# A fused attention and feed-forward kernel: the last pairs' work behind the first late pair's x pieces

## The chip, the cores and the metric

The kernel runs on one core of a Trainium2 chip. The metric is the device time of one execution in microseconds (us). Before the change it was 1020.24 us, the median of three runs (1018.71 to 1024.19).

## The reference, cut to what matters

```
def phi(x):                                # q and k: 8 batches x 8 heads x 576 x 64
    proj = x @ w_phi                       # 64 -> 128 features
    proj = proj - max(abs(proj), axis=-1)
    return concat([exp(proj), exp(-proj)])
kv  = phi(k)^T v ;  z = sum(phi(k))        # per head
out = (phi(q) @ kv) / (phi(q) @ z + 1e-6)
x   = out as 4608 tokens x 512
h   = x @ w_in                             # 512 -> 2048
g   = max(h, 0) + alpha * min(h, 0)
return g @ w_out                           # 2048 -> 512
```

## The kernel before, in words

**Attention phase.** Two heads make a pair; there are 32 pairs, 0 to 31. A pair goes through slots: its features are projected (`pj`, `pl`), centred on VectorE (DVE), exponentiated on ScalarE (ACT), multiplied (`kv`, `n`, `d`), and its numerator `s` is copied by ACT. The denominator `ds` takes a way of its own: SyncE (SP) writes it out as 9 values per partition, DVE inverts it (`r9`), SP stores and reloads it spread over the partitions (`rec_d`, then `rr`), GpSimd (POOL) multiplies `s` by `rr` (function `finish`), and SP stores the product into `x_d` (`store`). Beside that, POOL, ACT and DVE decode the weights and split every number into a high part (a cast to fp32r) and a low part (a subtraction), so that each product is three matmuls: high by high, low by high, high by low. In the same phase the first 512 tokens go through the feed-forward layer (`h`, `o`, `os`); their rows of `x_d` are read back (`xr`), cast by ACT and given low parts by POOL (`first_x`).

**Late phase.** The other 4096 tokens are four late pairs of 512-token chunks, p = 1 to 4. For each, seven combinations of blocks (a Strassen-like scheme: A11, A12, S1 to S4, A22) replace eight. `prepare` loads x rows (`xr`, two loads j = 0 and 1 of 1 MB, issued by POOL) and makes the 14 pieces `xo`: a subtraction if need be, a cast (ACT), a low part (DVE; for p = 1 and j = 1 POOL). Then eight units multiply them by w_in (`pa`, `pb`, `pc`; `begin`, `second`, `rest`, `end`), and `down_pair` multiplies by w_out (`qa`, `qb`, `qc`), adds up and stores output tiles (`give`). The pieces for p + 1 are made while pair p runs.

**What sets the order.** Up to the turn to the late phase every step is put at a place in a list: slot plus an offset from the table `OFF` (one column per kind of slot). Each of the five engines executes its steps in the order of that list. An engine never skips ahead: SP waits for a store's data before it issues the load behind it, POOL waits for `rr` before a low part that stands behind the multiplication. TensorE (PE) has places of its own (`PE_AT`, `FIRST`). In the late phase PE, SP and POOL follow the order in the code; DVE and ACT are ordered by a scheduler when the program is built.

Names used below: `s28` is the numerator of pair 28, `rr28` its spread reciprocal; `xo1_7_1` is the low or high part of piece 7 (S4) of late pair 1, half j = 1, `xo1_1_1` that of piece 1 (A22); `xr2_0` are the rows of late pair 2, half 0. Line 225 is the low part, 221 the cast, 580 the multiplication by `rr`, 777 the load of `xr`, 743 the store of an output tile, 809 to 811 the three matmuls of a late product, 437 the projection, 509 the last transpose of q, 662 the sum `os`.

Of the kernel before, what the change touches and what calls it, by code (L numbers as in the profile page):

```python
# [8 lines left out]
F32 = mybir.dt.float32  # L9
# [7 lines left out]
P = 128  # L17
# [19 lines left out]
UX, UH = 2, 0  # L37
PIECES = [(k, u) for k in range(1, 7) for u in range(NU)][3 : 3 + 45 : 3]
# [33 lines left out]
    ds=(14.33, 13.3, 7.99, 15.45, 13.27, 9.58),
    d9=(16.85, 17.98, 14.45, 17.7, 21.14, 20.67),
    dv=(5.89, 1.69, 8.95, 10.25, 13.98, 16.22),
    rd=(10.99, 12.64, 11.51, 16.79, 32.02, 21.63),
    rr=(17.22, 17.27, 24.13, 23.33, 40.33, 27.36),
    x=(22.95, 34.89, 31.98, 25.08, 41.28, 35.09),
    xs=(14.53, 27.34, 32.32, 34.7, 31.02, 35.64),
    load=(11.94, 16.85, 8.08, 15.36, 6.2, 15.96),
    scale=(8.31, 4.75, 6.13, 7.61, 3.27, 8.3),  # L80
    split=(10.48, 10.24, 9.28, 10.06, 10.86, 11.57),
    rest=(12.11, 11.81, 10.23, 10.08, 13.2, 12.51),
    add=(13.68, 15.29, 13.93, 15.13, 16.68, 13.36),
    high=(16.18, 17.39, 22.06, 16.52, 18.18, 17.09),
    low=(25.11, 17.99, 23.95, 16.85, 21.91, 23.14),
    store=(35.74, 50.42, 20.3, 10.28, 50.84, 20.57),
    sum0=(20.35, 11.48, 6.28, 10.58, 10.81, 8.43),
    sum1=(25.64, 12.1, 7.59, 11.85, 12.61, 11.64),
    sum2=(29.45, 17.95, 14.72, 20.15, 16.27, 13.45),
    sum3=(35.42, 19.51, 23.09, 22.37, 20.63, 15.46),  # L90
    sum4=(45.71, 24.55, 30.48, 31.06, 27.55, 30.01),
# [12 lines left out]
    cx0=(10.38, 5.5, 5.5, 17.0, 5.5, 5.5),
    cx1=(14.08, 6.0, 6.0, 17.95, 6.0, 6.0),
    cx2=(18.53, 7.0, 7.0, 18.55, 7.0, 7.0),
    cx3=(18.59, 7.5, 7.5, 19.84, 7.5, 7.5),
    lx0=(22.77, 7.0, 7.0, 17.54, 7.0, 7.0),
    lx1=(17.8, 7.1, 7.1, 21.69, 7.1, 7.1),
    lx2=(21.35, 8.1, 8.1, 22.98, 8.1, 8.1),  # L110
    lx3=(22.81, 8.2, 8.2, 21.47, 8.2, 8.2),
    al=(-136.86, 8.5, 8.5, -54.87, 8.5, 8.5),
    pt0=(5.56, 5.6, 5.6, 10.71, 5.6, 5.6),
    pt1=(7.23, 6.3, 6.3, 12.6, 6.3, 6.3),
    pt2=(7.5, 7.0, 7.0, 14.91, 7.0, 7.0),
# [89 lines left out]
def fused_kernel(ctx: ExitStack, tc: tile.TileContext, kq, v, w_phi, w_in, w_out, alpha, out):  # L205
# [211 lines left out]
    def attention_units(i):  # L417
# [190 lines left out]
        put(i + 2, "x", finish)  # L608
        put(i + 3, "xs", store)
# [157 lines left out]
    def prepare(p):  # L767
        c = 2 * p - 1
        todo = []
        for j in range(2):  # L770
# [162 lines left out]
    def down_pair(p):  # L933
# [4 lines left out]
        for k, n in enumerate(ORDER):  # L938
# [4 lines left out]
            for u in range(NU):  # L943
# [4 lines left out]
                for m in range(2):  # L948
# [9 lines left out]
                    if u == NU - 1:  # L958
                        ps = bk[key, m]
                        if n == A11:  # L960
                            bk["b", m] = bank(1, f"qb{p}_{m}")
                            act.copy(bk["b", m], ps)
                            continue
                        i = goal[n][0] + m, goal[n][1]
                        cuts = (0, C2 // 2, C2) if last_pair and m and n == A22 else (0, C2)
                        if i in part:
                            added(part[i], ps, part[i])
                            give(*i, part[i])
                            continue
                        x = part[i] = out_tile(*i)  # L970
                        for a, b in zip(cuts, cuts[1:]):
                            if a:
                                dve.tensor_copy(x[:, a:b], ps[:, a:b])
                            else:
                                act.copy(x[:, a:b], ps[:, a:b])  # L975
                            if n in (A12, A22):
                                give(*i, x, (a, b))
# [12 lines left out]
    with tc.manual_schedule(engines={et.PE, et.SP, et.Pool}):  # L990
        for n, bufs in (("hv", 1), ("gs", 1), ("wv", 1)):
            late[n] = ctx.enter_context(tc.tile_pool(name=n + "p", bufs=bufs, reuse_waits="tile"))
        for p in range(1, NC2 // 2 + 1):
            more_pairs = p < NC2 // 2
            queue += [(p, k, u) for k in range(len(ORDER)) for u in range(NU)]
            for u in range(NU):
                if u == UX and more_pairs:
                    prep += prepare(p + 1)
                    pieces(1)
# [19 lines left out]
            if more_pairs:  # L1019
                load_up(p + 1, 0)  # L1020
# [43 lines left out]
```

## Time and profile before

| | |
|---|---|
| median of three runs | 1020.24 us |
| profiled execution | 1020.62 us, span 1018.8 us |
| PE busy | 997.8 us, 98% of the span |
| DVE, ACT, POOL busy | 72%, 59%, 28% |
| mean granted PE clock | 0.996 |

The profile cuts the span into 40 slices. PE is at 9 tenths or more in all but the first, the sixteenth (some 382 to 407 us) and the last; the granted clock is below 9 tenths only in the seventeenth (407 to 433 us). DMA engines are 60 to 80% busy in the attention phase. A wait costs the whole kernel something only if PE stands still for it; so the view of what PE waited for comes first, and the order of instructions around each of those waits second.

### The profile page before, as it was taken

The page shows a single profiled execution, that of the slowest core. Times are in us where ns is not written, and L with a number is a line of the kernel's source. Part 1 is how long each engine was busy: PE and PEld are TensorE (multiplying, and loading weights), DVE is VectorE, ACT ScalarE, POOL GpSimd, SP SyncE. Part 2 cuts the span into 40 slices and gives each one's busy share as a digit, 9 for nine tenths or more (in the row PEclk, how much of TensorE's full clock was granted, in tenths as well). Part 3 has the DMA queues.
Part 4 walks back from the last instruction along what each step waited for, and adds up shares of the span by engine and source line. Part 5 has one row for each costly group of instructions (what it writes and reads, how often), then busy time and mean ns, then how long its engine had stood idle before and what let it go on. Part 6 is the DMA issues. An engine that isn't in the chain of part 4 may idle for free. (4 is left out here: it accounts for less than half of the span.)

```text
span 1018.8 us, 20525 instructions
## 1 busy us (share of the span) xinstructions
PE 997.8 (98%) x8142; PEld 803.8 (79%) x8142; DVE 736.7 (72%) x1106; ACT 597.1 (59%) x1051; POOL 283.1 (28%) x255
## 2 busy tenths in 40 slices
PE   8999999999999998999999999999999999999997
PEld 7777777777777775888888788888788888888886
DVE  7898788989898666657963657973566973565863
ACT  5887777677676665446653446654445653444552
POOL 0478767878787426000001000001000001000001
PEclk9999999999999999899999999999999999999999
DMA  6689887888887876547666557666556666454564
GB/s 200 182 281 306 272 263 240 283 278 271 299 269 263 258 235 206 202 177 254 236 218 224 198 193 250 230 213 228 190 213 248 223 211 218 168 212 176 186 211 141
DMA packets 106512, 232.41 MB, mean 228 GB/s; under 512 B 16944, under 2 KB 37808, under 8 KB 100272
## 3 DMA queue, kind: packets, MB, share of 16 engines
q1 hardware_dynamic: 101376, 214.24, 63.1%
q0 software_dynamic: 4752, 16.78, 4.5%
q8 instruction: 65, 1.06, 0.4%
q14 instruction: 31, 0.25, 0.1%
q10 hardware_dynamic: 288, 0.07, 0.0%
HBM read 182.53 MB, written 48.38 MB: 227 GB/s over the span
## 5 line engine op out<-in xcount | busy, mean ns | idle before, releaser
L221 ACT CAST hv<-g 128x512 fp32r<-128x512 f32 x224 | 139.2, 623 | 121.8 <-DVE hv L225 60.4
L225 DVE TENSOR_TENSOR hv<-g,hv 128x512 fp32r<-128x512 f32 x224 | 153.8, 695 | 73.0 <-ACT hv L221 72.5
L743 POOL DMA_DIRECT2D out_dram<-pt x33 | 18.0, 546 | 355.0 <-ACT pt L975 273.3
L809 PE MATMUL qa<-hv,wv 128*128 128x512 f32 x256 | 99.6, 389 | 0.0
L810 PE MATMUL qa<-hv,wv 128*128 128x512 f32 x256 | 99.6, 389 | 0.0
L811 PE MATMUL qa<-hv,wv 128*128 128x512 f32 x256 | 99.6, 389 | 0.0
L456 DVE TENSOR_REDUCE m<-pj 128x8 f32<-128x1024 f32 x64 | 77.3, 1208 | 30.4 <-PE pj L437 30.3
L475 ACT ACTIVATE xk<-t 128x1024 f32<-128x1024 f32 x64 | 67.2, 1062 | 34.4 <-DVE t L457 34.4
L457 DVE TENSOR_TENSOR t<-pj,m 128x1024 f32<-128x1024 f32 x64 | 78.4, 1225 | 4.1 <-ACT xk L475 0.4
L485 PE MATMUL kv<-v,xk 128*64 128x65 f32 x2048 | 78.0, 223 | 0.0
L485 PEld LDWEIGHTS kv<-v,xk 128*64 128x64 f32 x2048 | 70.7, 138 | 4.0 <-issue 0.3
L437 PEld LDWEIGHTS pj<-w_sb,raw 64*128 64x128 f32 x1024 | 60.0, 188 | 13.0 <-issue 6.7
L777 POOL DMA_DIRECT2D xr<-x_d x8 | 6.0, 755 | 230.8 <-DVE xo L225 230.4
L437 PE MATMUL pj<-w_sb,raw 64*128 64x128 f32 x1024 | 66.7, 279 | 2.7 <-DVE os L662 1.4
L531 PE MATMUL n<-qf,sf 128*64 128x288 f32 x512 | 68.2, 407 | 0.6 <-issue 0.5
L829 ACT ACTIVATE r<-g 128x512 f32<-128x512 f32 x65 | 37.6, 625 | 51.2 <-DVE g L825 51.2
L292 POOL TENSOR_TENSOR a<-e,a 128x512 f32<-128x512 f32 x32 | 44.6, 1394 | 79.5 <-DVE e L288 78.9
L830 DVE SCALAR_TENSOR_TENSOR g<-r,aln,g 128x512 f32<-128x512 f32 x65 | 48.5, 783 | 19.6 <-ACT r L829 19.6
L580 POOL TENSOR_TENSOR s<-s,rr 128x576 f32<-128x576 f32 x32 | 47.8, 1495 | 36.7 <-DMA rr<-rec_d 29.6
L811 PEld LDWEIGHTS qa<-hv,wv 128*128 128x128 f32 x256 | 48.0, 188 | 10.2
L810 PEld LDWEIGHTS qa<-hv,wv 128*128 128x128 f32 x256 | 48.1, 188 | 10.0
L809 PEld LDWEIGHTS qa<-hv,wv 128*128 128x128 f32 x256 | 48.1, 188 | 9.8
(147 smaller groups left out, 2585.9 us busy)
## 6 DMA issues: line engine op xcount, KB each, us to landing
ws<-us_d SPq DMA_DIRECT2D x32, 1024.0 KB
wv<-vs_d SPq DMA_DIRECT2D x64, 512.0 KB
wv<-v_d SPq DMA_DIRECT2D x48, 512.0 KB
raw<-kq_dram SPq DMA_DIRECT2D x31, 576.0 KB
wa<-u_d SPq DMA_DIRECT2D x32, 512.0 KB
v<-v_dram SPq DMA_DIRECT2D x32, 320.0 KB
rr<-rec_d SPq DMA_DIRECT2D x64, 144.0 KB
x_d<-s SPq DMA_DIRECT2D x32, 288.0 KB
```

The lines of the kernel that those rows point to most:

```text
L221: return act.copy(dst, src)
L225: return eng.tensor_tensor(dst, src, f(hi), op=ALU.subtract)
L437: pe.matmul(dst, lhsT=c["raw"][hs, j * P : (j + 1) * P], rhs=w_sb[hs], start=True, stop=True)
L456: dve.tensor_reduce(m, src, axis=AX.X, op=ALU.max, apply_absolute_value=True)
L457: dve.tensor_tensor(dst, src, m.unsqueeze(3).broadcast_to([P, nh, nj, FD]), op=ALU.subtract)
L475: act.activation(c["x", 0][:, n], c["t", 0], AF.Exp, scale=(1.0, -1.0)[n])
L485: pe.matmul(t[D * g : D * g + D, a, h * (D + 1) : (h + 1) * (D + 1)], lhsT=c["x", ch][:, a, h, j, D * g : D * g + D], rhs=c["v"][:, n : n ...
L531: pe.matmul(ps[D * h : D * h + D, :], lhsT=c["st"][:, a, D * h + 1 : D * h + D + 1], rhs=c["qf"][:, h, a, u * HS : (u + 1) * HS], start=a ...
L809: pe.matmul(ps, lhsT=wh, rhs=xh, start=first, stop=False, skip_group_check=True)
L810: pe.matmul(ps, lhsT=wl, rhs=xh, start=False, stop=False, skip_group_check=True)
L811: pe.matmul(ps, lhsT=wh, rhs=xl, start=False, stop=end, skip_group_check=True)
L830: dve.scalar_tensor_tensor(g, r, al1[:, ff : ff + 1], src, op0=ALU.mult, op1=ALU.add)
```

## The change

It has five parts.

1. The table `OFF` has new numbers for nearly all steps of ACT, DVE, POOL and SP in the attention phase; `finish` and `store` of the last five pairs (27 to 31) get entries of their own. PE's order is the same, instruction for instruction.
2. In `prepare` for p = 1 the low part of a piece is put behind the cast of the next piece (`behind`).
3. The rows of late pair p + 1 are asked for in the down phase of pair p (`PIECES` begins with (0, 3)) and no longer in its third unit (`UX`).
4. The last pair's last output tiles leave on SP's and ACT's queues and no longer on POOL's; the last half tile has a tile of its own (`y_end`).
5. `give` has an argument for the queue.

```
-UX, UH = 2, 0
-PIECES = [(k, u) for k in range(1, 7) for u in range(NU)][3 : 3 + 45 : 3]
+PIECES = [(0, 3)] + [(k, u) for k in range(1, 7) for u in range(NU)][3 : 3 + 45 : 3]
...
-    cx0=(10.38, 5.5, 5.5, 17.0, 5.5, 5.5),
+    cx0=(13.63, 5.5, 5.5, 17.0, 5.5, 5.5),
...
+    x_e31=(49.08, 49.08, 49.08, 215.43, 49.08, 49.08),
+    xs_e31=(58.7, 58.7, 58.7, 243.8, 58.7, 58.7),
...
-        put(i + 2, "x", finish)
-        put(i + 3, "xs", store)
+        e = f"e{i}" if i >= NPAIR - 5 else 0
+        put(i + 2, "x", finish, e)
+        put(i + 3, "xs", store, e)
...
-    def give(m, c, t, cuts=(0, C2)):
+    def give(m, c, t, cuts=(0, C2), queue=pool):
         for a, b in zip(cuts, cuts[1:]):
-            pool.dma_start(out[m * P : (m + 1) * P, c * C2 + a : c * C2 + b], t[:, a:b])
+            queue.dma_start(out[m * P : (m + 1) * P, c * C2 + a : c * C2 + b], t[:, a:b])
...
-                low(pool if p == 1 and j else dve, t[:, 1], b[src], t[:, 0])
+                behind.append(lambda: low(pool if p == 1 and j else dve, t[:, 1], b[src], t[:, 0]))
                 xo[p, n, j] = (t[:, 0], t[:, 1])
+                made[0] += 1
+                while len(behind) > int(p == 1 and made[0] < 14):
+                    behind.pop(0)()
...
-                        cuts = (0, C2 // 2, C2) if last_pair and m and n == A22 else (0, C2)
...
+                        if last_pair and m and n == A22:
+                            half, y = C2 // 2, late["cp"].tile([P, C2], F32, tag="cp", name="y_end", bufs=6)
+                            act.copy(x[:, :half], ps[:, :half])
+                            dve.tensor_copy(y[:, half:], ps[:, half:])
+                            give(*i, x, (0, half), act)
+                            give(*i, y, (half, C2), nc.sync)
+                            continue
+                        act.copy(x, ps)
+                        if n in (A12, A22):
+                            give(*i, x, queue=nc.sync if last_pair and n == A22 else pool)
...
-                if u == UX and more_pairs:
-                    prep += prepare(p + 1)
-                    pieces(1)
...
             if more_pairs:
+                prep += prepare(p + 1)
                 load_up(p + 1, 0)
```

POOL at the turn to the late phase, before:

```order
L580 TENSOR_TENSOR s28_5563<-s28_5563,rr28_5719 128x576
L225 TENSOR_TENSOR xo1_4_1_5783<-xr1_1_5463,xo1_4_1_5783 128x512
L580 TENSOR_TENSOR s29_5694<-s29_5694,rr29_5786 128x576
L580 TENSOR_TENSOR s30_5752<-s30_5752,rr30_5803 128x576
L225 TENSOR_TENSOR xo1_7_1_5810<-xr1_1_5463,xo1_7_1_5810 128x512
L777 DMA xr2_0_5986<-x_d_57 128x2x1024
L580 TENSOR_TENSOR s31_5800<-s31_5800,rr31_5814 128x576
L225 TENSOR_TENSOR xo1_1_1_5825<-xr1_1_5463,xo1_1_1_5825 128x512
L777 DMA xr2_1_6579<-x_d_57 128x2x1024
```

And now:

```order
L234 TENSOR_TENSOR xo1_4_1_5784<-xr1_1_5464,xo1_4_1_5784 128x512
L589 TENSOR_TENSOR s28_5471<-s28_5471,rr28_5716 128x576
L589 TENSOR_TENSOR s29_5618<-s29_5618,rr29_5780 128x576
L589 TENSOR_TENSOR s30_5719<-s30_5719,rr30_5799 128x576
L234 TENSOR_TENSOR xo1_7_1_5802<-xr1_1_5464,xo1_7_1_5802 128x512
L234 TENSOR_TENSOR xo1_1_1_5819<-xr1_1_5464,xo1_1_1_5819 128x512
L787 DMA xr2_0_6489<-x_d_57 128x2x1024
L589 TENSOR_TENSOR s31_5787<-s31_5787,rr31_5809 128x576
L787 DMA xr2_1_6579<-x_d_57 128x2x1024
```

The multiplication of pair 28 went behind piece 4; that of pair 31, and the load of `xr2_0`, went behind the last piece, `xo1_1_1`. The multiplications of pairs 28 to 30 still stand ahead of piece 7.

ACT where the first 512 tokens' rows (`xr0`) are cast to `x0`, before:

```order
L273 ACTIVATE a1_1_1338<-raw2_1_1206 128x512
L221 CAST x0_0_1359<-xr0_0_1315 128x512
L541 COPY s6_1366<-n6_1306 128x576
L221 CAST x0_1_1395<-xr0_0_1315 128x512
L558 ACTIVATE ds6_1397<-d6_1326 128x288
```

And now:

```order
L282 ACTIVATE a1_1_1356<-raw2_1_1140 128x512
L550 COPY s6_1363<-n6_1314 128x576
L567 ACTIVATE ds6_1365<-d6_1331 128x288
L504 COPY sf7_1368<-kv7_1254 128x260
L528 ACTIVATE qf8_1371<-qt8_1_1344 128x512 x2
L528 ACTIVATE qf8_1371<-qt8_0_1343 128x512 x2
L532 ACTIVATE qf8_1371<-q28_1353 128x2x64 x2
L230 CAST x0_0_1380<-xr0_0_1299 128x512
L230 CAST x0_1_1382<-xr0_0_1299 128x512
```

The two casts went behind the copy of the denominator (`ds6`) and the exponentials of q (`qf8`).

DVE where the sums of the first chunk's outputs meet the projection of pair 16, before:

```order
L372 SCALAR_TENSOR_TENSOR g0_5_2576<-r0_5_2575,aln_81,g0_5_2576 128x512
L662 TENSOR_TENSOR os0_2_2145<-o0_1_2_2659,os0_2_2145 128x512
L662 TENSOR_TENSOR os0_3_2188<-o0_1_3_2666,os0_3_2188 128x512
L456 TENSOR_REDUCE m16_0_2726<-pj16_0_2700 128x8
L457 TENSOR_TENSOR t16_0_2725<-pj16_0_2700,m16_0_2726 128x1024
```

And now:

```order
L672 TENSOR_TENSOR os0_3_2221<-o0_1_3_2660,os0_3_2221 128x512
L672 TENSOR_TENSOR os0_2_2147<-o0_1_2_2653,os0_2_2147 128x512
L576 RECIPROCAL r9_12_2728<-d9_12_2595 128x9
L465 TENSOR_REDUCE m16_0_2774<-pj16_0_2692 128x8
L466 TENSOR_TENSOR t16_0_2773<-pj16_0_2692,m16_0_2774 128x1024
```

The two sums changed places (the bank of `o0_1_3` is the one that `pj16_0` is written to next), and the reciprocal of pair 12, which stood ahead of the decoding steps, comes behind them.

## Rows read from the trace of the kernel before

**Rows 1.** The page: busy time, and granted clock in 40 slices

```profile
PE 997.8 (98%) x8142; PEld 803.8 (79%) x8142; DVE 736.7 (72%) x1106; ACT 597.1 (59%) x1051; POOL 283.1 (28%) x255
...
PEclk9999999999999999899999999999999999999999
```

**Rows 2.** Waits of PE, longest in total first: us, times, longest

```profile
PE pa L811 <- POOL xo L225: 3.4, 1, 3.4
...
PE q L509 <- ACT ds L558: 2.1, 1, 2.1
PE pj L437 <- DVE os L662: 1.4, 3, 0.5
```

**Rows 3.** Windows of 2 us: engines' busy time, granted clock, DMA share, GB/s

```profile
408.00:410.00 2.00, 2.00 (x5) 1.61 (x6) 0.95 (x2) 0.60 (x1) 0.00 (x0) 0.50 0.94 330
410.00:412.00 2.00, 2.00 (x6) 1.52 (x6) 0.00 (x0) 0.60 (x1) 0.00 (x0) 0.50 0.98 386
412.00:414.00 2.00, 2.00 (x7) 1.56 (x6) 1.29 (x3) 0.19 (x1) 0.00 (x0) 0.53 0.78 227
```

**Rows 4.** Timeline at the turn: start, us, engine, line, operation [idle before, releaser]

```profile
399.15 0.62 ACT L221 CAST xo<-xr 128x512 fp32r<-128x512 f32 x1 [0.28 <-DVE xr L786]
399.26 1.82 POOL L580 TENSOR_TENSOR s<-s,rr 128x576 f32<-128x576 f32 x1 [3.05 <-DMA rr<-rec_d]
...
401.04 1.71 POOL L225 TENSOR_TENSOR xo<-xr,xo 128x512 fp32r<-128x512 f32 x1
...
402.70 0.76 POOL L777 DMA_DIRECT2D xr<-x_d  x1
...
402.81 0.50 PE L811 MATMUL pc<-xo,ws 128*128 128x512 f32 x1 [0.94 <-POOL xo L225]
...
404.07 0.40 PE L810 MATMUL pa<-xo,wb 128*128 128x512 f32 x1
...
406.10 1.70 POOL L225 TENSOR_TENSOR xo<-xr,xo 128x512 fp32r<-128x512 f32 x1
...
407.86 0.80 PE L811 MATMUL pa<-xo,wb 128*128 128x512 f32 x1 [3.39 <-POOL xo L225]
...
412.71 0.69 DVE L786 TENSOR_TENSOR t<-xr 128x512 f32<-128x512 f32 x1 [3.76 <-DMA xr<-x_d]
```

**Rows 5.** Timeline in late pair 2: load of pair 3's rows, DVE and PE behind it

```profile
555.81 0.72 POOL L777 DMA_DIRECT2D xr<-x_d  x1
...
563.74 0.69 DVE L786 TENSOR_TENSOR t<-xr 128x512 f32<-128x512 f32 x1 [3.13 <-DMA xr<-x_d]
...
568.78 0.50 PE L809 MATMUL pa<-xo,ws 128*128 128x512 f32 x1 [0.81 <-ACT u L821]
```

**Rows 6.** Timeline where the first chunk's x rows are cast

```profile
81.73 0.62 ACT L221 CAST x<-xr 128x512 fp32r<-128x512 f32 x1 [1.43 <-DMA xr<-x_d]
...
83.77 0.44 PE L509 MATMUL q<-ident,t 128*128 128x128 f32 x2 [2.05 <-ACT ds L558]
...
89.00 3.93 POOL L225 TENSOR_TENSOR x<-xr,x 128x512 fp32r<-128x512 f32 x3
...
93.62 0.40 PE L618 MATMUL h<-x,wo 128*128 128x512 f32 x1
```

**Rows 7.** Timeline where PE waits for the sum of the first chunk's outputs

```profile
176.59 1.28 DVE L662 TENSOR_TENSOR os<-o,os 128x512 f32<-128x512 f32 x2
...
177.92 2.06 PE L437 MATMUL pj<-w_sb,raw 64*128 64x128 f32 x32 [0.51 <-DVE os L662]
```

**Rows 8.** Timeline at the end

```profile
1013.02 0.39 PE L811 MATMUL qa<-hv,wv 128*128 128x512 f32 x1
1013.64 1.60 POOL L743 DMA_DIRECT2D out_dram<-pt  x3 [9.03 <-ACT pt L975]
1013.85 0.42 DVE L973 COPY pt<-qa 128x256 f32<-128x256 f32 x1 [5.86 <-ACT pt L975]
```

**Rows 9.** Waits of POOL

```profile
POOL s L580 <- DMA rr<-rec_d: 29.6, 7, 19.8
```

More of the change, by code (lines that the diff above doesn't have):

```diff
@@ L72 @@
[L72 to L91, printed above, removed]
@@ new lines @@
+    mq=(5.65, 8.07, 3.52, 6.75, 7.22, 3.12),
+    mt=(4.86, 2.88, 2.46, 6.03, 5.06, 2.97),
+    ke0=(3.3, 5.91, 6.78, 6.85, 8.67, 6.12),
+    ke1=(5.41, 6.03, 12.54, 11.88, 8.79, 12.37),
+    ke2=(7.09, 8.35, 7.1, 9.5, 14.22, 12.93),
+    kc=(12.14, 13.05, 8.76, 6.89, 12.71, 14.18),
+    qe=(13.33, 9.13, 10.11, 16.92, 10.06, 14.93),
+    s=(11.27, 6.54, 7.74, 13.22, 9.42, 8.5),
+    ds=(11.47, 8.24, 8.89, 15.42, 9.64, 11.15),
+    d9=(14.54, 19.27, 17.56, 21.35, 21.96, 21.93),
+    dv=(5.45, 11.6, 15.99, 14.46, 14.76, 11.65),
@@ new lines @@
+    rd=(7.95, 21.83, 17.98, 16.47, 24.89, 20.99),
+    rr=(15.39, 26.39, 27.13, 26.0, 34.39, 24.65),
+    x=(24.48, 35.74, 28.84, 25.08, 42.2, 28.46),
+    xs=(13.16, 28.07, 34.55, 29.11, 32.66, 36.9),
+    load=(3.65, 1.17, 13.81, 15.36, 7.54, -0.66),
+    scale=(8.93, 2.88, 5.69, 7.61, 0.04, 2.07),
+    split=(10.5, 10.82, 9.19, 10.06, 8.58, 11.96),
+    rest=(13.41, 11.6, 9.29, 10.08, 11.25, 13.83),
+    add=(14.55, 13.93, 15.05, 15.13, 17.01, 13.92),
+    high=(16.77, 15.99, 18.22, 16.52, 18.82, 17.92),
@@ new lines @@
+    low=(23.03, 18.12, 20.12, 16.85, 22.67, 18.1),
+    store=(49.69, 30.27, 48.27, 10.28, 57.31, 24.73),
+    sum0=(23.02, 9.13, 9.24, 10.58, 6.74, 9.22),
+    sum1=(26.57, 12.92, 14.6, 11.85, 7.93, 13.07),
+    sum2=(29.05, 14.4, 15.42, 20.15, 14.93, 15.86),
+    sum3=(35.6, 21.69, 17.89, 22.37, 21.99, 19.22),
+    sum4=(46.26, 28.41, 23.63, 31.06, 29.31, 32.32),
+    glu0=(12.7, 23.39, 10.84, 12.7, 20.72, 14.29),
+    glu1=(13.8, 23.55, 12.6, 13.8, 32.16, 24.23),
+    glu2=(0.5, 0.54, 18.6, 0.5, 13.11, 18.71),
@@ new lines @@
+    cx2=(14.97, 7.0, 7.0, 18.55, 7.0, 7.0),
+    cx3=(19.44, 7.5, 7.5, 19.84, 7.5, 7.5),
+    lx0=(15.22, 7.0, 7.0, 17.54, 7.0, 7.0),
+    lx1=(17.22, 7.1, 7.1, 21.69, 7.1, 7.1),
+    lx2=(19.11, 8.1, 8.1, 22.98, 8.1, 8.1),
+    lx3=(20.55, 8.2, 8.2, 21.47, 8.2, 8.2),
+    al=(-60.47, 8.5, 8.5, -54.87, 8.5, 8.5),
+    pt0=(5.56, 5.6, 5.6, 8.67, 5.6, 5.6),
+    pt1=(7.23, 6.3, 6.3, 11.58, 6.3, 6.3),
+    pt2=(7.5, 7.0, 7.0, 12.6, 7.0, 7.0),
+    pt3=(12.61, 11.2, 11.2, 17.37, 11.2, 11.2),
+    pt4=(12.93, 13.6, 13.6, 19.64, 13.6, 13.6),
@@ new lines @@
+    pt5=(18.82, 16.0, 16.0, 22.15, 16.0, 16.0),
+    pt6=(23.73, 18.3, 18.3, 30.05, 18.3, 18.3),
+    pt7=(26.97, 20.7, 20.7, 36.21, 20.7, 20.7),
+    pt8=(31.93, 23.1, 23.1, 36.99, 23.1, 23.1),
+    pt9=(37.24, 25.5, 25.5, 44.62, 25.5, 25.5),
+    pt10=(46.04, 27.9, 27.9, 45.2, 27.9, 27.9),
+    pt11=(48.22, 30.2, 30.2, 54.91, 30.2, 30.2),
+    pt12=(54.07, 32.6, 32.6, 65.15, 32.6, 32.6),
+    pt13=(95.83, 35.0, 35.0, 68.21, 35.0, 35.0),
+    pt14=(130.31, 37.4, 37.4, 118.78, 37.4, 37.4),
+    pt15=(177.59, 39.8, 39.8, 119.13, 39.8, 39.8),
@@ new lines @@
+    lu0=(16.03, 6.0, 6.0, 4.97, 6.0, 6.0),
+    lu1=(25.62, 6.2, 6.2, 28.44, 6.2, 6.2),
+    mk_s0=(0.13, 1.4, 1.4, 1.4, 1.4, 1.4),
+    mt_s0=(3.74, 2.8, 2.8, 2.8, 2.8, 2.8),
+    mq_s0=(12.58, 4.2, 4.2, 4.2, 4.2, 4.2),
+    mk_s1=(1.09, -5.6, -5.6, -5.6, -5.6, -5.6),
+    mt_s1=(-1.15, -4.2, -4.2, -4.2, -4.2, -4.2),
+    mq_s1=(6.77, 2.1, 2.1, 2.1, 2.1, 2.1),
+    mk_s2=(1.68, -7.0, -7.0, -7.0, -7.0, -7.0),
+    mt_s2=(3.68, 0.84, 0.84, 0.84, 0.84, 0.84),
+    mq_s2=(9.27, 0.98, 0.98, 0.98, 0.98, 0.98),
@@ new lines @@
+    mk_s3=(-2.65, -6.3, -6.3, -6.3, -6.3, -6.3),
+    mq_s3=(5.67, 2.1, 2.1, 2.1, 2.1, 2.1),
+    mt_s3=(7.32, 3.5, 3.5, 3.5, 3.5, 3.5),
+    ke0_s3=(-0.74, -1.4, -1.4, -1.4, -1.4, -1.4),
+    ke1_s3=(0.32, 0.0, 0.0, 0.0, 0.0, 0.0),
+    ke2_s3=(10.9, 5.6, 5.6, 5.6, 5.6, 5.6),
+    ke0_s0=(6.38, 3.5, 3.5, 3.5, 3.5, 3.5),
+    ke1_s0=(7.57, 5.6, 5.6, 5.6, 5.6, 5.6),
+    ke2_s0=(9.81, 7.7, 7.7, 7.7, 7.7, 7.7),
+    kc_s0=(0.57, 0.7, 0.7, 0.7, 0.7, 0.7),
+    ke0_s1=(1.78, 0.84, 0.84, 0.84, 0.84, 0.84),
@@ new lines @@
+    ke1_s1=(5.55, 1.4, 1.4, 1.4, 1.4, 1.4),
+    ke2_s1=(-0.64, 2.1, 2.1, 2.1, 2.1, 2.1),
+    qe_s0=(26.95, 18.2, 18.2, 18.2, 18.2, 18.2),
+    kc_s1=(4.39, -1.4, -1.4, -1.4, -1.4, -1.4),
+    qe_s1=(25.24, 23.1, 23.1, 23.1, 23.1, 23.1),
+    ke0_s2=(2.19, -0.7, -0.7, -0.7, -0.7, -0.7),
+    ke1_s2=(5.62, 0.0, 0.0, 0.0, 0.0, 0.0),
+    ke2_s2=(8.73, 2.8, 2.8, 2.8, 2.8, 2.8),
+    s_s0=(2.74, 3.5, 3.5, 3.5, 3.5, 3.5),
+    ds_s0=(6.19, 6.3, 6.3, 6.3, 6.3, 6.3),
+    qe_s2=(12.08, 11.9, 11.9, 11.9, 11.9, 11.9),
@@ L768, in prepare @@
         c = 2 * p - 1
-        todo = []
+        todo, behind, made = [], [], [0]
         for j in range(2):
@@ L970, in down_pair @@
                         x = part[i] = out_tile(*i)
[L971 to L977, printed above, removed]
+                        if last_pair and m and n == A22:
[8 more added lines that the diff above has]
+                            give(*i, x, queue=nc.sync if last_pair and n == A22 else pool)
     ahead = unit(1, 0)
```

111 lines of the change are left out of this document (26 added, 85 removed).

## The prediction

> **What bounds the kernel now.** I read the page first, then what PE waited for, then the timeline around each long wait with the order of the engines beside it. PE is busy for 997.8 of the span's 1018.8 us [rows 1], and this change leaves its instructions and their order alone. So it can gain only where PE stands still or runs at half clock, and it can lose wherever a moved step makes PE stand still anew. The list of PE's waits [rows 2] shows the few places: 3.4 us for one low part from POOL, 2.1 us for a denominator on ACT, 1.4 us in three pieces for the sums `os` on DVE.
>
> The largest is the turn to the late phase [rows 4]. POOL executes in order, and low parts that PE needs stand behind multiplications that nobody needs yet. The multiplication at 399.26 (`s30`) stood 3.05 us for `rr`; so the low part of piece 7 began only at 401.04, though its cast, which reads unsubtracted rows, did not wait for that, and PE waited 0.94 us until 402.81. Then POOL issued the load of pair 2's rows (402.70), waited for `rr31`, multiplied, and began the low part of the last piece, A22, at 406.10; PE waited 3.39 us until 407.86. The cast for this one was done at 399.15 + 0.62 = 399.77: POOL's order alone made it late. After the stop the windows from 408 to 414 show a granted clock of 0.50, 0.50 and 0.53 [rows 3]; 0.50 is the 1.2 GHz level. These six us did the work of 2 x 0.50 + 2 x 0.50 + 2 x 0.53 = 3.06 us, a loss of 2.94. The turn thus costs 0.94 + 3.39 + 2.94 = 7.27 us.
>
> **The change part by part.**
>
> *POOL at the turn.* `xo1_1_1` now follows `xo1_7_1`, ahead of the load and of `s31`. `s30` is still ahead of `xo1_7_1`, and the requests that lead to `rr30` hardly move, so I leave that wait at 0.94. POOL then ends `xo1_7_1` at 401.04 + 1.71 = 402.75 and `xo1_1_1` 1.70 later, at 404.45. PE's matmul before the one that reads it starts at 404.07, and the next would follow 0.25 later (the five from 402.81 to 404.07 come 0.25 apart), at 404.32; with the signal between the engines about 0.2 us of waiting is left of 3.39. With so short stops I expect no fall of the clock: after the stop of 2.05 us at 83.77 [rows 6] the slice of the page stays at 9 [rows 1]. So 7.27 - 0.94 - 0.2 = 6.1 us come free here, if nothing else is late.
>
> *What is late next: the rows of pair 2.* Their load is issued at about 404.5 and no longer at 402.70, while PE is some 7 us ahead. DVE has subtractions on these rows in its order; the scheduler put them five rows later than before, behind the sum on S3 of unit 1. Before, DVE stood 3.76 us until 412.71, 10.0 us after the issue [rows 4]; PE, at half clock, didn't feel it. In pair 2 DVE stood 3.13 us and PE lost 0.81 through ACT's copy `u` [rows 5]: some 2.3 us of DVE's standing are covered. Now PE goes through A12, S2, S1 and S3 of unit 1 (24 matmuls at 0.25) from 404.5 to 410.5, DVE ends the sum (0.7 us) at about 411.4, and the rows land between 404.5 + 7.9 = 412.4 (7.9 is pair 2's load, 555.81 to 563.74) and 414.5 (10.0 as before). DVE stands 1.0 to 3.1 us, PE 0 to 0.8. I take 0.6, nearer the upper end, as the crowd of loads is the same as before. Turn: 6.1 - 0.6 = 5.5 us. Bounds: 7.3 if nothing at all is late, 0 if another stop is as long and the clock falls again.
>
> *Low parts one piece later.* For pair 1 a subtraction and its cast get ahead of the preceding low part, by one DVE or POOL step. No wait of PE hangs on it but those above: nothing, and 0.7 us (one step of DVE) on either side.
>
> *Rows asked for in the down phase.* On POOL the loads for pairs 3 and 4 stand where they stood, behind the last output tiles of the pair before, and DVE's subtractions on them too. The load at 555.81 and the 0.81 us of PE behind it stay [rows 5]. Nothing.
>
> *The casts of the first chunk's rows.* ACT stood 1.43 us for the rows before the cast at 81.73; the copy of the denominator was behind it, and PE waited 2.05 us for the bank [rows 6]. The casts now follow that copy and q's exponentials, which hides their wait for the DMA. Next in line are the low parts that the first product `h` reads: POOL ended them at 89.00 + 3.93 = 92.93, and the first matmul on one started at 93.62. With PE 2.05 us earlier it comes at 91.57; POOL no longer puts two half-width sums of weights between these low parts; at a low part's 1.3 us for both it would be done near 91.6. That just fits: 1.9 us, between 0 and 2.05.
>
> *The sums `os`.* Two of them took 1.28 us, and PE waited 0.51 for the second, whose bank `pj16` needs [rows 7]. Now the needed one is first, 0.64 us earlier: the wait goes. The same exchange stands at a second of the three waits; at the third only a reciprocal leaves the way. I count 1.0 of 1.4 us; bounds 0 and 1.4.
>
> *The end.* PE's last matmul begins at 1013.02 and takes 0.39. POOL issued three stores from 1013.64 to 1015.24, and DVE's copy began only at 1013.85 because it stood behind ACT's copy into the same tile [rows 8]. With a tile of its own it starts about 0.4 earlier, and three stores on two other queues end their issue near 1014.3: 0.9 us. What follows an issue stays. Bounds 0 and 1.6, POOL's whole issue time. The Trainium skill (Trainium Kernel Development and Optimization, Key Constraints) says that issuing from several engines only saves the sequencer's issue time, since all use the same DMA engines. It also gives (DMA: Bandwidth & Descriptors, Latency and other measured facts) a first byte after about 1 us by GpSimd's queue and 0.6 by the others, so by the page's figures the gain would be an estimated 1.3 us. No run here shows a store of the hardware queues at the end.
>
> *The rest of the table.* Some 600 rows of ACT, DVE, POOL and SP change places. The list of PE's waits holds nothing longer than those named [rows 2], so little can be won: 1.5 us, as much as a wait below the named ones could come to. Lost can be two new waits like that at 83.77, 4.1. I take 0.
>
> Sum: 5.5 + 1.9 + 1.0 + 0.9 = 9.3 us. From the profiled execution's 1020.62 (its span plus 1.8 around it) that gives 1011.3. The median of the runs is 0.38 below that execution, so 1011.0.
>
> **The rivals.**
>
> *The rows of pair 2 take the wait over.* If their load takes longer than 10 us in the crowd of weight loads (DMA share 0.94 and 0.98 in [rows 3]), each us more on DVE is one on PE. At 12.5 us DVE stands 5.6 and PE 3.3, as long as the stop that is removed, and the clock falls: 6.1 - 3.3 - 2.9 leaves nothing at the turn. Time: 1011.0 + 5.5 = 1016.5, no change that can be told. For it: PE comes 7 us earlier and the load 1.8 later. Against it: one landing took 7.9.
>
> *Late reciprocals stop POOL: slower.* Many `RECIPROCAL` rows go behind 4 or 5 others on DVE. Then `rec_d` and `rr` come some 4 us later, and the multiplication on POOL stands for `rr` with the low parts `gl` behind it, which PE's products of the first chunk need. POOL stood 29.6 us for `rr` already, 19.8 of it at one place [rows 9]. The multiplications moved back by 2 or 3 rows of 1.3 us, about as much, which speaks against it. If it were 0.7 us of PE in each of the 21 slots of the first chunk, it would cost 14.7: 1011.0 + 14.7 = 1025.7, slower. It decides from 0.45 us a slot, where the gain is gone.
>
> *Everything fits.* `rr30` lands sooner because the store of `s28` no longer goes ahead of it, piece 7 isn't late, and the rows come in time: 0.94 + 0.2 + 0.6 more, 1009.3; with the upper bounds of the other parts 1007.
>
> **How the numbers follow.** A difference of 0.5% (5.1 us: below 1015.1, above 1025.3) is about what can be told from no change here. The forecast, with one or two us on either side, gets 0.66; everything fits 0.12; the rows of pair 2, or a few new waits of the table that come to as much, 0.17; late reciprocals 0.05. That makes faster 0.78, same 0.17, slower 0.05. The range goes from 1006.5 (all bounds) to 1017.5, just past the first rival; the forecast's own is 1008.5 to 1014.
>
> **What would show it.** Right: no wait `pa L811 <- POOL xo` over 0.5 us, a granted clock of 1.00 through the turn, no wait `q L509 <- ACT ds`, waits of `pj` on `os` below 0.5 in total, waits `pa L809 <- ACT u` for pairs 3 and 4 still there at about 2 us, the last stores issued within 1 us of PE's last matmul. Wrong: a new wait over 2 us of PE on ACT or DVE in unit 1 or 2 of the first late pair with the clock at half, or PE below 24 of 25 us in windows of the attention phase that were full.

## The result and the profile after

The changed kernel takes 1011.2 us, the median of four runs (1010.7 to 1011.9), beside 1021.3 of the kernel before in the same session (1018.7 to 1024.2): a ratio of 0.990, interval 0.987 to 0.993. The prediction was 1011.0, 1006.5 to 1017.5. The profiled execution has a span of 1009.7 us and took 1011.5.

The page of the changed kernel; its lines answer to [rows 1]:

```profile
PE 995.9 (99%) x8142; PEld 801.9 (79%) x8142; DVE 739.5 (73%) x1106; ACT 597.6 (59%) x1051; POOL 282.1 (28%) x252
...
PEclk9999999999999999999999999999999999999999
```

The slice with the low clock is gone. What PE waited for (line numbers are 9 to 13 higher than before), beside [rows 2]:

```profile
PE pa L822 <- ACT u L834: 3.7, 3, 1.7
...
PE pc L824 <- POOL xo L234: 0.9, 1, 0.9
...
PE q L518 <- ACT ds L567: 0.6, 1, 0.6
PE qt L515 <- DVE t L466: 0.4, 1, 0.4
...
PE pc L822 <- DVE g L838: 0.4, 1, 0.4
PE pj L446 <- DVE os L672: 0.3, 1, 0.3
```

The 3.4 us for a low part of POOL is gone, and `os` fell from 1.4 to 0.3. `ds` fell from 2.1 to only 0.6, and a 0.4 for `t` is new ahead of it (in a second execution of this kernel neither is over 0.1; see the store of the weight sums below). The wait for ACT's `u` grew from 2.1 in two waits to 3.7 in three: the third is new, at the turn. The timeline there, beside [rows 4]:

```profile
395.47 1.56 POOL L589 TENSOR_TENSOR s<-s,rr 128x576 f32<-128x576 f32 x1 [2.08 <-DMA rr<-rec_d]
...
396.99 3.43 POOL L234 TENSOR_TENSOR xo<-xr,xo 128x512 fp32r<-128x512 f32 x2
...
398.77 0.50 PE L824 MATMUL pc<-xo,ws 128*128 128x512 f32 x1 [0.89 <-POOL xo L234]
...
400.35 0.76 POOL L787 DMA_DIRECT2D xr<-x_d  x1
...
400.47 0.50 PE L824 MATMUL pa<-xo,wb 128*128 128x512 f32 x1
...
411.18 0.69 DVE L796 TENSOR_TENSOR t<-xr 128x512 f32<-128x512 f32 x1 [2.88 <-DMA xr<-x_d]
411.91 0.69 DVE L796 TENSOR_TENSOR t<-xr,t 128x512 f32<-128x512 f32 x1
...
412.52 0.69 DVE L796 TENSOR_TENSOR xr<-xr 128x512 f32<-128x512 f32 x1
...
413.12 0.68 DVE L838 TENSOR_TENSOR g<-pc,u 128x512 f32<-128x512 f32 x1
...
413.86 0.50 PE L822 MATMUL pc<-xo,ws 128*128 128x512 f32 x1 [0.38 <-DVE g L838]
...
414.56 1.42 DVE L843 SCALAR_TENSOR_TENSOR g<-r,aln,g 128x512 f32<-128x512 f32 x2 [0.76 <-ACT r L842]
...
417.20 0.50 PE L822 MATMUL pa<-xo,ws 128*128 128x512 f32 x1 [1.68 <-ACT u L834]
```

The two last low parts now stand together, and the matmul that waited 3.39 us [rows 4] starts 0.19 us late (400.47; the ones before it come 0.24 apart). The rows of pair 2 are asked for behind them and land 10.8 us after the issue. DVE stands 2.88 us for them, three subtractions follow, then the sum on S4, and PE waits 0.38 for that sum and 1.68 for the copy `u` behind it.

PE executes the same matmuls in the same order in both kernels, so the start of one in the profile before less its start after is PE's lead at that place. Its changes are the ledger of the 9.04 us between the two spans (1018.76 and 1009.71). The lead counts somewhat more than the lists of waits, since a short delay of PE is not in them.

| Stretch | PE's lead, us | change | predicted |
|---|---|---|---|
| start, to 75 us | 0 to -0.33 | -0.33 | 0 |
| casts of the first chunk's rows, to 94 us | to 0.18 | +0.51 | 1.9 |
| waits for `os`, at 178, 231, 284 us | | +1.17 | 1.0 |
| other waits, to 402 us | to 3.99 | +2.64 | 0 |
| turn: stop and half clock gone | to 10.20 | +6.21 | 6.1 |
| turn: new waits | to 7.34 | -2.86 | -0.6 |
| late phase, to PE's last matmul | to 7.43 | +0.09 | 0 |
| from PE's last matmul to the end | | +1.61 | 0.9 |
| sum | | 9.04 | 9.3 |

Of the "other waits" 2.5 us are four of the list before, all below 0.75 us: 0.70 for keys (`raw`) at 373 us, 0.53 at 379, 0.48 and 0.16 for `t` at 304 and 251. The total was right; four of its terms were not, and their misses cancel. The ledger is that of one execution of each kernel.

### The profile page after: what moved, and what is told of

Read it like the earlier page. It is cut to its first block, busy times and chain, and to the rows that moved or that the text cites. A ratio compares the mean times of both kernels' runs of the same rounds, so it can differ in the third digit from the quotient of the medians.

```text
span 1009.7 us, 20556 instructions
## 1 busy us (share of the span) xinstructions
PE 995.9 (99%) x8142; PEld 801.9 (79%) x8142; DVE 739.5 (73%) x1106; ACT 597.6 (59%) x1051; POOL 282.1 (28%) x252
## 3 DMA queue, kind: packets, MB, share of 16 engines
q8 instruction: 65, 1.06, 0.4%
```

## The experiments

Each is an edit of the changed kernel unless said otherwise. Where one execution is set beside another, the lead of PE is taken as above.

**The turn put back.** The last five pairs get common offsets again:

```
-    x=(24.48, 35.74, 28.84, 25.08, 42.2, 28.46),
-    xs=(13.16, 28.07, 34.55, 29.11, 32.66, 36.9),
+    x=(24.48, 35.74, 28.84, 26.05, 42.2, 28.46),
+    xs=(13.16, 28.07, 34.55, 34.7, 32.66, 36.9),
...
-        put(i + 2, "x", finish, e)
-        put(i + 3, "xs", store, e)
+        put(i + 2, "x", finish)
+        put(i + 3, "xs", store)
```

> The changed kernel, with the last five pairs' multiplications and stores back at common offsets: on POOL the load of xr2_0, s31 and the other multiplications stand ahead of the low parts of pieces 7 and A22 again; all else as changed. Theory: the order on POOL is what the turn gained. Then PE waits 3 us or more for a low part of POOL at the turn, the granted clock falls to about 0.5 for some us behind it, the 1.7 us wait on ACT's u goes (the rows of pair 2 are asked for earlier), and the time is 3 to 7 us above the changed kernel's 1011.2 (1014 to 1018). Rival: the turn gained from the rest of the table (earlier reciprocals and loads): no such wait, clock 1.00, time within 1.5 us of 1011.2.

Measured: 1015.6 us (eight runs), ratio to before 0.994 to 0.997. Its longest waits of PE:

```profile
PE pc L813 <- POOL xo L224: 5.3, 1, 5.3
PE pa L811 <- ACT u L823: 1.7, 2, 1.5
PE pa L813 <- POOL xo L224: 1.5, 2, 1.0
```

and its windows of 2 us at the turn (columns as in [rows 3]):

```profile
402.00:404.00 2.00, 0.00 (x0) 0.00 (x0) 0.00 (x0) 0.00 (x0) 1.17 (x1) 1.00 0.93 344
404.00:406.00 2.00, 0.51 (x1) 0.50 (x2) 0.00 (x0) 0.00 (x0) 2.00 (x3) 0.64 0.82 330
406.00:408.00 2.00, 2.00 (x6) 1.52 (x5) 1.64 (x3) 0.95 (x2) 0.68 (x1) 0.50 0.49 107
408.00:410.00 2.00, 2.00 (x6) 1.51 (x6) 2.00 (x4) 0.50 (x2) 0.00 (x0) 0.50 0.92 385
```

The wait on POOL is back, longer since PE arrives sooner; the clock falls to 0.50 behind it; and the new wait at the turn goes: the rows are asked for 1.1 us sooner (399.22) and land after 7.3 us, while PE is late by the stop. So the order of these steps is what the turn gained, by stop and clock, and the new wait is its price. On SP the stores of these pairs and loads of `rr` move with POOL's steps here; the test does not part the two.

**The end, the two halves of the edit apart.** Once the stores on POOL's queue again, once one tile again:

```
-                            give(*i, x, (0, half), act)
-                            give(*i, y, (half, C2), nc.sync)
+                            give(*i, x, (0, half))
+                            give(*i, y, (half, C2))
...
-                            give(*i, x, queue=nc.sync if last_pair and n == A22 else pool)
+                            give(*i, x)
```

> The changed kernel with its last three stores on POOL's queue again; the tile of its own for the last half stays. Theory: the end's gain is the queues' alone: from PE's last matmul to the end of the span 5.8 us as in the kernel before, where the changed one has 4.1; time 1012.8. Rival: the tile of its own is what gained: 4.1 to 4.5 us, time 1011.2 to 1011.6.

```
-                            half, y = C2 // 2, late["cp"].tile([P, C2], F32, tag="cp", name="y_end", bufs=6)
+                            half, y = C2 // 2, x
```

> The changed kernel with one tile for both halves of the last output tile; the new queues stay. Theory: DVE's copy starts behind ACT's in either case, so the tile is worth nothing: 4.1 us from PE's last matmul to the end, time 1011.2. Rival: the tile lets DVE's copy go beside ACT's and is worth 0.4 us: 4.5 us, time 1011.6.

Measured: 1012.9 and 1010.7 us. From the start of PE's last matmul to the end of the span the first needs 1011.88 - 1006.12 = 5.76 us, the second 1011.35 - 1007.23 = 4.12, the changed kernel 1009.71 - 1005.59 = 4.12, the kernel before 1018.76 - 1013.02 = 5.74 [rows 8]. The end of the changed kernel:

```profile
1005.59 0.39 PE L824 MATMUL qa<-hv,wv 128*128 128x512 f32 x1
...
1006.01 0.37 ACT L985 COPY pt<-qa 128x256 f32<-128x256 f32 x1
1006.42 0.35 ACTq L753 DMA_DIRECT2D out_dram<-pt  x1
1006.42 0.42 DVE L986 COPY y_end<-qa 128x256 f32<-128x256 f32 x1 [5.85 <-ACT pt L985]
1006.87 0.35 SPq L753 DMA_DIRECT2D out_dram<-y_end  x1
```

DVE's copy still starts 0.83 us after PE's last matmul, behind ACT's, as before: both read one bank of the accumulators. The queues gained all of it: 0.6 us as the last issue ends 1.63 us after that matmul instead of 2.22, and 1.0 us as the end comes 2.5 us after the last issue instead of 3.5. The two experiments agree: 3.5 on POOL's queue, 2.5 on SP's.

**The casts of the first chunk's rows, put back in the changed kernel and made alone in the kernel before.** First:

```
-    fx=(3.37, 0.2, 0.2, 10.59, 0.2, 0.2),
-    cx0=(13.63, 5.5, 5.5, 17.0, 5.5, 5.5),
+    fx=(5.58, 0.2, 0.2, 10.59, 0.2, 0.2),
+    cx0=(10.38, 5.5, 5.5, 17.0, 5.5, 5.5),
...
```

> The changed kernel with the old offsets of the load, casts and low parts of the first chunk's rows: ACT's first cast stands ahead of s6 and ds6 again, SP loads the rows behind two other loads. Theory: the casts' place is worth what their wait costs: PE's wait for ds comes back at 2 us or more (0.58 in the changed kernel), time 1012.2 to 1014. Rival: what PE gains there it loses at the low parts before the first product h, so PE's lead behind that product is the same within 0.3 us, time 1011.2.

Measured: 1018.3 us (ten runs), far over what was expected; the one longest wait of PE:

```profile
PE q L518 <- ACT ds L567: 8.0, 1, 8.0
```

With the old offset SP's load of the rows falls behind two others in the new table, and ACT, with `ds` behind the cast, stands until it lands. The windows from 88 to 94 us are at a clock of 0.50. The edit does what it was meant to do; this kernel does not price it, since the load moved too.

Then, in the kernel before, the casts alone (the new offsets of casts and low parts, cx0 and cx1 at 14.6 and 14.7 so that they stand behind its `qf8`):

```
-    cx0=(10.38, 5.5, 5.5, 17.0, 5.5, 5.5),
-    cx1=(14.08, 6.0, 6.0, 17.95, 6.0, 6.0),
+    cx0=(14.6, 5.5, 5.5, 17.0, 5.5, 5.5),
+    cx1=(14.7, 6.0, 6.0, 17.95, 6.0, 6.0),
...
```

> The kernel before with one edit of the change alone: the casts of the first chunk's rows stand on ACT behind ds6 and q's exponentials, and their low parts on POOL ahead of two sums; SP's order is the old one. Theory: the prediction's price of this edit was right by itself, and in the changed kernel the late store of the weight sums took it: PE's wait of 2.05 us for ds falls below 0.3, PE is 1.5 to 2.05 us earlier behind the first product h, time 1018.4 beside 1020.3 of before. Rival: the low parts are late for h, PE gives back most of it there: 0.7 us or less.

Measured: 1019.4 us (ten runs), ratio 0.997 to 1.000. The wait for `ds` is gone and PE's lead over the kernel before is 2.01 us at 82 us, as predicted. PE gives it back in two places: to 1.39 at a load of `v`, and from 1.32 to 0.16 at the first products:

```profile
PE h L618 <- POOL x L225: 0.9, 1, 0.9
...
PE kv L485 <- DMA v<-v_dram: 0.6, 1, 0.6
```

The second is the rival. In this kernel the last of the four low parts still stands behind two half-width sums on POOL (it starts at 91.59); in the changed kernel all four stand ahead of them.

**The store of the weight sums sooner.** In the changed kernel ACT's cast of the next sums, in the slot before, waits for the store that empties its tile:

```profile
77.56 1.04 ACT L230 CAST sd<-a 128x1024 fp32r<-128x1024 f32 x1 [2.62 <-DMA us_d<-sd]
...
82.65 0.41 ACT L567 ACTIVATE ds<-d 128x288 f32<-128x288 f32 x1
```

SP issues that store at 67.45 us, behind two loads, and at 65.77 in the kernel before. The edit puts it ahead of the loads and moves no other step:

```
-    sum4=(46.26, 28.41, 23.63, 31.06, 29.31, 32.32),
+    sum4=(44.5, 28.41, 23.63, 31.06, 29.31, 32.32),
```

> The changed kernel with one number changed: the store of the weight sums (us_d from sd) stands on SP ahead of the loads raw and raw of keys again, as in the kernel before. Theory: ACT's 2.62 us stand at the cast of the next sums (77.56), which waits for that store, is what makes ds late now: it goes, PE's wait for ds (0.58) and the 0.45 for t fall below 0.3 together, time 1010.6 (1010.2 to 1010.9). Rival: ds waits for other work on ACT: wait and time as in the changed kernel, 1011.2.

Measured: 1009.6 us, but the ratio to before (0.988 to 0.993) is that of the changed kernel; the trace decides. The cast starts at 74.49 and waits for nothing, both waits of PE are gone, and PE's lead over the changed kernel grows by 1.4 us, from 0.27 at 8 us to 1.67 at 95. With the 0.5 of the ledger that is 1.9 for the casts and this store together, as much as was predicted for the casts. But one execution does not give the size. In the changed kernel's second execution (below) ACT stood less for the store, and PE waited 0.09 us for `ds` and not for `t`:

```profile
77.08 1.05 ACT L230 CAST sd<-a 128x1024 fp32r<-128x1024 f32 x1 [1.65 <-DMA us_d<-sd]
```

In the eight kept executions with the casts in their new place and the store late, ACT stood 1.65 to 3.07 us and PE's lead over the kernel before grew by 0.1 to 1.6 us between 75 and 95 us (0.5 and 1.6 in the changed kernel's own two); in the three with the store sooner ACT did not stand, and it grew by 1.8 to 2.2. The groups don't meet, so the theory holds.

**Three subtractions of pairs 2 to 4 on POOL.**

```
-                    dve.tensor_tensor(b[dst], b[x], b[y], op=ALU.subtract)
+                    (pool if p > 1 and j == 0 and n != A22 else dve).tensor_tensor(b[dst], b[x], b[y], op=ALU.subtract)
...
-            todo.insert(j, load)
+            todo.insert(7 if p > 1 and j else j, load)
```

> The changed kernel with the first three subtractions on half 0's rows of late pairs 2, 3 and 4 on POOL and no longer on DVE (and the load of half 1 asked for behind six pieces, since POOL executes in order); the loads of half 0 are issued where they were. Theory: PE's waits at the head of the late pairs (1.68 and 0.38 us in pair 1, 0.75 in pair 2, 1.31 in pair 3, 4.1 in all) come from DVE standing in order for rows that have not landed; with POOL standing in its place they go, below 0.5 us in total, and the time is 1011.2 - 3.7 = 1007.5 (1006.5 to 1008.5). Rival: ACT's copies and DVE's sums are late there on their own account: waits stay, 1010.5 to 1011.5. Second rival: POOL's slower subtractions make pieces late or slow DVE down: new waits on POOL's or DVE's steps, 1011 or more.

Measured: 1008.7 us, ratio 0.985 to 0.991, which meets the changed kernel's; the trace decides. POOL now stands for the rows, 8.59 us at pair 2, and what is left in the late phase is:

```profile
PE pc L824 <- POOL xo L234: 1.8, 1, 1.8
...
PE pa L822 <- ACT u L834: 0.6, 1, 0.6
...
PE pa L822 <- DVE g L838: 0.5, 1, 0.5
PE pc L822 <- ACT p L834: 0.3, 1, 0.3
```

The waits for `p` (at 396.53 us) and for POOL (at 399.81) lie ahead of the rows' load (400.95), so only 0.55 + 0.46 = 1.0 us follow the rows, instead of 4.1 (0.75 + 1.31 + 1.68 + 0.38). That DVE's standing in order makes these waits is shown; the gain is 3.1 by them, and PE's lead over the changed kernel grows by 2.9 from 410 us to the end, not by 3.7. The profiled execution hides it: its wait for piece 7's low part, which stands behind `s30` on POOL, is 1.83 us, twice the changed kernel's 0.89; the clock in the windows of 2 us from 400 on falls to 0.50 and 0.77; and its 1010.6 us are the longest of four. Nothing in the edit stands ahead of that wait.

**Pair 30's multiplication later.**

```
-    x_e30=(62.08, 62.08, 62.08, 69.86, 62.08, 62.08),
+    x_e30=(62.08, 62.08, 62.08, 216.0, 62.08, 62.08),
```

> The changed kernel with one number changed: the multiplication of pair 30 stands behind both last low parts and the load of xr2_0 on POOL, beside that of pair 31. Theory: the 0.89 us for piece 7 and the 0.2 for piece A22 come from s30's wait for rr30 alone: both go, and the load is issued some 3 us sooner, so that the waits of 1.68 and 0.38 shrink to 1 us or less: 1009.2 (1008.5 to 1010.2). Rival: DVE's subtractions move two steps forward with the sooner load, and DVE stands as long as before: 1010.2 to 1011.2.

Measured: 1012.6 us, above theory and rival, and slower than the changed kernel (1011.2), though ratios overlap. (In this kernel and in the first of the parts together pair 30 is stored ahead of its multiplication, so the division of that pair is left out.) Both waits for POOL go and the load is issued at 396.81, 3.5 us sooner. But DVE's subtractions, ordered by an estimate of when the rows land, moved forward two rows:

```profile
396.81 0.76 POOL L787 DMA_DIRECT2D xr<-x_d  x1
...
408.06 0.69 DVE L796 TENSOR_TENSOR t<-xr 128x512 f32<-128x512 f32 x1 [4.03 <-DMA xr<-x_d]
...
411.34 0.77 PE L822 MATMUL pa<-xo,wb 128*128 128x512 f32 x1 [3.43 <-DVE g L838]
```

The rows landed 11.25 us after the issue, DVE stood 4.03 us, PE 3.43, and the window from 412 to 414 is at 0.50: the very thing that the prediction's first rival described.

**The parts together**, first with that fault, then with pair 30's store moved behind its multiplication, beside the changed kernel once more:

```
-    x_e30=(62.08, 62.08, 62.08, 69.86, 62.08, 62.08),
-    xs_e30=(71.7, 71.7, 71.7, 147.21, 71.7, 71.7),
+    x_e30=(62.08, 62.08, 62.08, 214.0, 62.08, 62.08),
+    xs_e30=(71.7, 71.7, 71.7, 243.0, 71.7, 71.7),
...
-                            act.copy(x[:, :half], ps[:, :half])
-                            dve.tensor_copy(y[:, half:], ps[:, half:])
+                            act.copy(x, ps)
```

> The changed kernel with all of these together: three subtractions of pairs 2 to 4 on POOL (-3.7), s30 later (-1.1), the store of the weight sums sooner (-0.6), and at the end one copy of the last tile by ACT in place of two half copies one behind the other, in two stores (-0.2). Theory: the parts are independent: 1011.2 - 5.6 = 1005.6 (1004.5 to 1007). Rival: with PE earlier the next wait takes their place (low parts of POOL, or the rows of half 1): 1008 or more.

> The changed kernel once more, unaltered, beside the next two: how much the waits at the late pairs' heads vary between executions. Expected 1011.2 (1010.2 to 1012), three waits for ACT's u at pairs 1, 2 and 3 between 0.5 and 2 us each.

> The changed kernel with three subtractions of pairs 2 to 4 on POOL, pair 30's multiplication behind both last low parts with its store moved behind it, the store of the weight sums sooner, and one copy at the end: as in the run of the parts together, but with pair 30's store in its right place. Theory: the store's place touches no wait of PE: span 1005.0 as there, time 1006.5 (1004.5 to 1008). Rival: with s30 and its store beside s31 the load of xr2_0 waits for them and pair 2's rows are late again: 1008 or more.

Measured: 1007.3 (above the range expected), 1011.8 and 1006.4 us; the last two, of one session, have ratios of 0.9899 to 0.9928 and 0.9848 to 0.9881, which do not meet. So the third kernel beats both: 14 us below the kernel before, 5 below the changed one. Its longest waits of PE on the late pairs:

```profile
PE pc L822 <- ACT p L834: 0.6, 1, 0.6
PE pa L822 <- DVE g L838: 0.5, 1, 0.5
PE pa L822 <- ACT u L834: 0.5, 1, 0.5
```

In the changed kernel's second execution the waits for `u` come to 3.2 us, each within 0.5 of the first's.

**One subtraction ahead of the sum.** Of the three at pair 2, two on POOL:

```
-                    dve.tensor_tensor(b[dst], b[x], b[y], op=ALU.subtract)
+                    (pool if p == 2 and j == 0 and n in (S2, S3) else dve).tensor_tensor(b[dst], b[x], b[y], op=ALU.subtract)
...
-            todo.insert(j, load)
+            todo.insert(7 if p == 2 and j else j, load)
```

> The changed kernel with two of the three subtractions on pair 2's half 0 on POOL: on DVE only one stands between the wait for the rows and the sum on S4 (as in pairs 3 and 4, where one stands there), where the changed kernel has all three. Theory: the prediction's landing was right and its cover wrong: in six executions PE lost DVE's standing less 0.8 to 0.9 us here, but less 2.3 us at pairs 3 and 4, and the difference is the two subtractions (2 x 0.6 us) ahead of the sum. Then with DVE standing 2.6 to 3.1 us PE loses 0.4 to 1.0 at pair 2 (2.06 in the changed kernel), time 1.1 to 1.5 us below 1011.2 (1009.7 to 1010.1). Rival: the cover is small since PE's schedule is tight in pair 1 whatever stands ahead of the sum: loss of 1.7 us or more, 1010.8 to 1011.5.

Measured: 1011.3 us (six runs, 1010.0 to 1016.4), no gain that can be told. In the profiled execution the rows came after 9.6 us, DVE stood 1.70 and PE lost 0.91. That is the standing less 0.8 again, so the larger cover did not show. But POOL's two subtractions ran beside DVE's next step:

```profile
410.81 0.68 DVE L838 TENSOR_TENSOR g<-pc,u 128x512 f32<-128x512 f32 x1
410.97 1.29 POOL L796 TENSOR_TENSOR t<-xr,t 128x512 f32<-128x512 f32 x1 [8.19 <-DVE t L796]
...
412.22 1.29 POOL L796 TENSOR_TENSOR xr<-xr 128x512 f32<-128x512 f32 x1
412.25 2.48 DVE L843 SCALAR_TENSOR_TENSOR g<-r,aln,g 128x512 f32<-128x512 f32 x2 [0.76 <-ACT r L842]
```

and that step took 2.48 us, where the changed kernel has 1.42. The 1.06 us eat most of what the 1.2 us of two subtractions would give. The test does not tell theory and rival apart.

## Why the prediction was right, and where its steps were not

The direction, the place of the largest gain and the total came out. That the total did is luck: the casts, the rows of pair 2 and the start brought 4.0 us less than predicted, the rest of the table and the end 3.4 more. Of the signs that it named, the wait for `ds` did not go in the first execution. Step by step:

- *POOL at the turn:* right. 0.94 stayed (0.89), about 0.2 was left of 3.39 (0.19), the clock stayed at 1.00; 6.2 us by the ledger for 6.1. Putting the order back brought stop and half clock back.
- *The rows of pair 2:* the mechanism and its place were right, the size was not: 0.6 expected, 2.06 measured in two waits, 2.9 by PE's lead. DVE's standing, 2.88 us, lay in its bounds (1.0 to 3.1); the landing, 10.8 us after the issue, was 0.8 past the upper end of its own. What failed is the cover of "some 2.3 us", carried over from pair 3's rows [rows 5]. In six executions with this order on DVE PE lost the standing less 0.5 to 0.8 here (1.98 us gave 1.45, 2.58 gave 1.75, 2.88 gave 2.06, 3.64 gave 2.82), and at the two later pairs the standing less 2.3 to 2.4 (2.60 gave 0.27, 3.07 gave 0.75, 4.40 gave 2.03). In DVE's order three subtractions stand between wait and sum here, one there; 2 x 0.6 us is most of the 1.5 between the covers. That this is the cause is argued from the order, not shown.
- *Low parts one piece later:* no wait of PE names a low part but the two at the turn. Not tried alone.
- *Rows asked for in the down phase:* nothing, as far as the traces tell. The two loads are issued at 548.48 and 702.65 us, before at 555.81 and 710.04, which is PE's lead of 7.3 and 7.4; the waits at pairs 3 and 4, 0.81 and 1.32 before, are 0.75 and 1.31. Not tried alone.
- *The casts:* 1.9 expected, 0.5 measured in the ledger, 0.1 to 1.6 over eight executions. The wait on the rows went, but the price stood on "what is late next" being only the low parts. The same table had put a store of the weight sums behind two loads, and ACT stood 2.62 us for it a slot earlier. With the store back the term is whole, 1.8 to 2.2. In the kernel before, a low part took more than half of it: the sentence that they "just fit" holds only with the new order of POOL.
- *The sums `os`:* 1.0 expected, 1.2 measured.
- *The end:* 0.9 expected, 1.6 measured, at the upper bound, which was POOL's issue time alone. The tile of its own gave nothing. The Trainium skill (PSUM — Partial Sum Buffer, PSUM bank collisions raise a hardware error) says that two engines at one bank at once, in the same group of 32 partitions, are an error, reads too, and that the compiler keeps them apart. In every profile with two copies DVE's starts behind ACT's, with one tile or with two, which agrees. What failed is "What follows an issue stays": a store on the other queues also ends sooner, 2.5 instead of 3.5 us after its issue, so 1.0 of the 1.6 is not issue time. The estimate that the prediction made from the Trainium skill (DMA: Bandwidth & Descriptors, Latency and other measured facts), 1.3, was nearer.
- *The rest of the table:* 0 expected, 2.6 measured, above the bound of 1.5. The four waits of 0.16 to 0.70 that went are rows of before's list; the prediction put them at nothing and followed no part of the diff to them. Which steps removed them stays open.

Of the rivals, late reciprocals did not come: no wait of PE on `gl` in the list, and POOL stood 27.0 us for `rr` where it stood 29.6. The rows of pair 2 took 2.9 of the turn's gain and not all of it.

## What to carry to other kernels

When a step leaves a queue, look up what else in the same edit moved on the engine that waited: a wait for a transfer ends at the next transfer, and the price of an edit is that of the whole new order. A cover read at one loop turn (2.3 us) need not hold at another (0.8); count there which instructions stand between the wait and the reader. One profiled execution does not price a wait: the same program waited 0.58 us for `ds` once and 0.09 once. And where a scheduler orders an engine by its own estimate of a transfer, asking for the data sooner also moves the reader forward; let an engine with time to spare stand for it.

## What the runs showed of the hardware that was not expected

- The same load of 1 MB took 9.6 to 11.6 us to land at the turn in the eight executions with the changed kernel's order there, and 7.2 to 8.7 at the two later pairs. Among the programs that differ only at the very end it varies by 1.1 and 1.3 us at one place.
- The length of a stop does not tell by itself whether the clock falls. Stops of PE of 2.03 us at pair 4 (in the kernel with one end tile) and of 1.83 at the turn (with three subtractions on POOL) were followed by a clock of 0.50 to 0.51, the 1.2 GHz level; one of 1.68 with 0.38 ahead of it, at the turn of the changed kernel, was not, nor was the one of 2.05 at 83.77 us in the kernel before (1.00 in the windows from 82 to 90). The first and the third, in windows of 2 us:

```profile
714.00:716.00 2.00, 0.27 (x1) 0.27 (x2) 2.00 (x4) 1.93 (x4) 0.00 (x0) 1.00 0.24 96
716.00:718.00 2.00, 2.00 (x6) 1.56 (x6) 1.03 (x2) 0.78 (x2) 0.00 (x0) 0.51 0.00 0
718.00:720.00 2.00, 2.00 (x7) 1.54 (x7) 1.13 (x2) 0.00 (x0) 0.00 (x0) 0.64 0.01 4
```

```profile
416.00:418.00 2.00, 0.80 (x4) 0.68 (x5) 2.00 (x4) 1.57 (x4) 0.00 (x0) 1.00 0.05 20
418.00:420.00 2.00, 2.00 (x10) 1.67 (x9) 1.55 (x3) 0.62 (x1) 0.00 (x0) 1.00 0.00 0
```

- A subtraction on POOL slows DVE's work beside it: 2.48 instead of 1.42 us for two joins, of which the one beside POOL took 1.81 and the other 0.74. The sum `g` from `pc`, which also had a subtraction on POOL beside it, took its usual 0.68; one of its two inputs lies in the accumulators. The Trainium skill (SBUF — State Buffer, SBUF: two separate sides) says that the two engines share a pair of ports, and that of a DVE instruction with two inputs in SBUF and a GpSimd one that reads SBUF the one that comes second waits until the other's is over. That agrees: the 1.06 us added are less than one POOL instruction of 1.29, and only the join had both inputs in SBUF.
